# Positive parts of one batch's late queries: from ScalarE out of PSUM to GpSimd out of SBUF, with all engine lists made anew

## Chip, cores, metric

The kernel runs on one core of a Trainium2 chip. The metric is the device time of one execution in microseconds (us). The engines are named as in the profile: PE (TensorE), PEld (its weight loads), DVE (VectorE), ACT (ScalarE), POOL (GpSimd), SP (the queue that issues most transfers).

## What is computed

Block-sparse causal attention, followed by a two-layer feed-forward block with an ELU. Batch is 4, heads 8, sequence 768, head width 64, and keys come in 24 chunks of 32.

```python
k_min = np.min(k_chunks, axis=3); k_max = np.max(k_chunks, axis=3)
ub = np.sum(np.maximum(q * k_min, q * k_max), axis=-1)     # query against every chunk
ub = np.where(causal, ub, -1e9)
top_chunks = np.argsort(ub, axis=-1)[..., -6:]             # six chunks for each query
scores = where(selected and causal, q @ k.T / 8, -1e9)
x = softmax(scores) @ v                                    # (3072, 512)
h = x @ w_in                                               # (3072, 2048)
out = where(h > 0, h, exp(min(h, 0)) - 1) @ w_out          # (3072, 512)
```

The upper bound is computed as `q @ k_min + max(q, 0) @ (k_max - k_min)`, which is where the positive part of the queries comes from.

## The kernel before

Two heads make a pair; a batch has pairs 0 to 3, and two pairs make a quad, for which the chunks are selected together. Batches 1 to 3 are prepared a whole pair at a time (`pair_prep`). Batch 0 alone (`SPLIT`) is cut into two halves of 384 queries, so that work can begin early, and prepared by `first_prep(u, hf)`. For each pair and half it does the following. Keys and queries arrive in the tile `gT`, used here as a staging buffer. PE transposes them (L696) into PSUM banks, keys as `psH`, queries as `psMT`. ACT copies the keys to `lhs` (L706), DVE takes minima and maxima by chunk (L715) and their difference (L722). ACT copies the transposed queries to the SBUF tile `f` (L728) and writes their positive part to the tile `qa` (L732), both out of the PSUM bank, which is free after the second. For the first half the positive part has 192 columns (queries below 192 need no selection), for the second half 384. POOL casts the queries from `f` to bf16 in `rhs` (L748) and the values to `vext` (L739).

`quad_sel` then computes the bounds on PE out of `f`, `qa` and the chunk tiles (L782, into a two-bank PSUM tile `psS`). DVE transposes them (L798), takes the eight largest of each row (L810), compares (L815) and transposes back (L821). POOL copies the outcome into extra rows of `rhs` (L832, four copies for a quad, two for each pair). `pair_attend` computes scores (L874, with products for the triangular mask at L880), which carry the selection through these rows; a score tile of a half's queries waits for both copies of its pair. ACT makes exponentials (L901), PE multiplies by the values (L933), DVE normalizes (L946, L949), PE transposes (L982) and ACT copies to `xT` (L985). `mlp` is the feed-forward part: L1011, ELU on ACT and DVE (L1020 to L1054), L1070, L1079. There are two `psS` tiles, and four banks for `psH`, `psMT` and the other single-bank tiles together.

The order of work is fixed in advance. Each step is an operation with a number in the order of `add`, and `QUEUE` holds for each engine the list of these numbers, written out by hand. Each engine works through its list in order and waits, at each operation, for what that one needs. A small planner (`Plan`) walks these lists with assumed durations to choose buffers; its constants (`PHASE`, the durations given to `add`) reach the chip only through that choice. The eight weight loads are issued by POOL within its list (L570, L574), and they and their number stand in it like any other operation.

Numbers that the diff's lists show, for batch 0's second half: key transposes 169, 185, 203, 219 and query transposes 175, 191, 209, 225 for pairs 0 to 3; query copies 176, 192, 210, 226; positive parts 177, 193, 211, 227; casts of queries 178 and 179, 194 and 195, 212 and 213, 228 and 229. Bounds of the first half are 81 and 122, of the second 231 and 281. The two selection copies of pair 0 for the second half are 237 and 238, of pair 1 239 and 240. The first scores of pair 0's second half are 241, 243, 245, 247 and 249, by key block, with exponentials 242 to 250. Weight issues are 331 to 345. Loads on SP: 217 is the query load of pair 3's second half, 197 a key load of that half, 517 and 519 the first key and query load of batch 1 (four starts each), 17, 51, 201 and 167 value loads (three starts each).

Of the kernel before, what the change touches and what calls it, by code (L numbers as in the profile page):

```python
# [85 lines left out]
    ],  # L86
    "ACT": [
# [19 lines left out]
    ],  # L107
# [7 lines left out]
    ],  # L115
# [42 lines left out]
class Plan:  # L158
# [17 lines left out]
    def add(self, eng, dur, prio, emit, reads=(), writes=(), alloc=(), free=(), lat=None, tag="",  # L176
# [32 lines left out]
        o.users = []  # L209
        o.followers = []  # L210
        self.ops.append(o)
        return o

    WINDOW = 3.4133
    PHASE = 0.77
    ENOUGH = 0.43

    def clocked(self, r, dur, act):

        w = int(math.floor((r - self.PHASE) / self.WINDOW)) + 1  # L220
        warm = w > 0 and act[w - 1] >= self.ENOUGH * self.WINDOW
# [931 lines left out]
```

## Time and profile before

| | |
|---|---|
| runs (3) | median 268.44 us, from 268.43 to 268.44 |
| the profiled execution | 268.42 us, of which the span shown is 266.7 us |
| busy in the span | PE 256.0, DVE 211.6, ACT 195.8, POOL 118.0 us |
| the four instructions that move | L732 ACT, 128x384, 511 ns mean |

Times in the profile are from the start of the span. A row of the timeline gives start, length, engine, line, operation, output and inputs, and in brackets the idle time before it with what ended it. A row of groups gives count, busy time, mean duration in ns, then idle time ahead and what ended it. Names are the program's, without buffer numbers, so `rhs` is the bf16 query tile, `lhs` the key tile and `f` any of a pool of fp32 tiles.

### The profile page before, as it was taken

What the parts mean: (1) busy time and instruction counts of PE and PEld (TensorE: products, weight loads), DVE (VectorE), ACT (ScalarE), POOL (GpSimd) and SP (SyncE); (2) the same over time, 40 slices, a digit from 0 to 9 for tenths busy, and PEclk for the clock granted to TensorE, in tenths of its full rate; (3) what the DMA queues carried; (4) which work ended last, traced back from release to release, by engine and by line L of the source; (5) the groups of instructions that cost most, each with busy time, mean ns of one, the idle gap of its engine ahead of it and who ended that gap; (6) DMA issues with size and microseconds to landing.
All of it is one profiled execution on the core that took longest, in us unless ns stands there. A gap on an engine that the chain in (4) does not pass through costs nothing.

```text
span 266.7 us, 6618 instructions
## 1 busy us (share of the span) xinstructions
PE 256.0 (96%) x2393; PEld 159.4 (60%) x2420; DVE 211.6 (79%) x544; ACT 195.8 (73%) x363; POOL 118.0 (44%) x208
## 2 busy tenths in 40 slices
PE   4999999999999999999999999999999999999994
PEld 3887766755565556655565555655666555565543
DVE  4897999999999999899997858986779676227640
ACT  4899899955987789997899549787988842433421
POOL 2588774163896898952934157524250000000000
PEclk9999999999999999999999999999999999999999
DMA  6999999999998999999403561040102300210123
GB/s 206 272 238 155 205 194 202 196 147 177 198 153 134 163 204 159 152 167 186 106 7 77 175 172 18 15 125 15 58 11 59 116 2 0 79 42 0 39 81 118
DMA packets 121264, 32.15 MB, mean 121 GB/s; under 512 B 108304, under 2 KB 118288, under 8 KB 121232
## 3 DMA queue, kind: packets, MB, share of 16 engines
q1 hardware_dynamic: 115920, 26.75, 51.3%
q0 software_dynamic: 4224, 4.19, 10.0%
q10 hardware_dynamic: 1088, 0.79, 0.9%
q8 instruction: 19, 0.31, 0.5%
q14 instruction: 13, 0.11, 0.2%
HBM read 28.44 MB, written 7.47 MB: 135 GB/s over the span
## 4 chain that ended last, share of the span: by engine, by line
PE 83%; DVE 5%; ACT 5%; DMA 4%; issue 2%; SPq 0%; DVEq 0%; ACTq 0%
PE psH L1011 20%; PE psM L1070 20%; PE psS L874 11%; PE psS L1011 8%; PE psMT L1070 8%; PE psO L933 7%; PE psS L782 3%; DMA f<-in_v_dram 3%; PE psH L696 2%; PE psMT L696 2%; ACT pt L901 2%; DMA gT<-in_k_dram 1%; ACT lhs L706 1%; PE psT L982 1%; DVE thr L810 1%
## 5 line engine op out<-in xcount | busy, mean ns | idle before, releaser
L901 ACT ACTIVATE pt<-psS 128x768 bf16<-128x768 f32 (+1 forms) x120 | 89.1, 778 | 11.9 <-PE psS L874 7.3
L1011 PE MATMUL psH<-xT,w_in_sb 128*128 128x384 bf16 x384 | 75.0, 326 | 0.3
L1070 PE MATMUL psM<-w_out_sb,gT 128*128 128x512 bf16 x264 | 67.9, 379 | 1.3
L1011 PEld LDWEIGHTS <-w_in_sb 128*128 128x128 bf16 x512 | 47.6, 97 | 34.4 <-issue 1.4
L1070 PEld LDWEIGHTS <-gT 128*128 128x128 bf16 x400 | 37.8, 98 | 34.4 <-DVE gT L1054 0.5
L1020 ACT ACTIVATE f<-psH 128x384 f32<-128x384 f32 x96 | 47.8, 509 | 12.5 <-PE psH L1011 10.1
L920 POOL TENSOR_SCALAR_AFFINE_SELECT pt<-pt 128x512 bf16<-128x512 bf16 (+1 forms) x48 | 24.8, 529 | 69.0 <-ACT pt L901 61.9
L874 PE MATMUL psS<-rhs,lhs 88*128 88x384 bf16 (+4 forms) x304 | 54.2, 283 | 0.8 <-ACT pt L901 0.6
L874 PEld LDWEIGHTS <-lhs 88*128 88x128 bf16 x304 | 27.9, 97 | 15.4 <-ACT pt L901 1.9
L1049 DVE SCALAR_TENSOR_TENSOR t<-f,psH 128x384 bf16<-128x384 f32 x56 | 30.5, 546 | 6.3 <-ACT f L1020 5.8
L748 POOL CAST rhs<-f 64x768 bf16<-64x768 f32 (+1 forms) x40 | 27.9, 702 | 14.1 <-DVE f L633 6.6
L933 PEld LDWEIGHTS <-pt 128*128 128x128 bf16 x672 | 27.5, 98 | 7.5 <-issue 0.9
L1054 DVE SCALAR_TENSOR_TENSOR gT<-psH,t 128x384 bf16<-128x384 f32 x56 | 30.6, 551 | 1.2
L933 PE MATMUL psO<-vext,pt 128*128 128x65 bf16 x672 | 29.6, 194 | 0.2 <-DVE gT L1054 0.2
L748 POOL CAST lhs<-f 64x768 bf16<-64x768 f32 x24 | 19.7, 822 | 18.6 <-PE psS L874 12.3
L832 POOL COPY rhs<-selt 24x576 bf16<-24x576 bf16 (+2 forms) x40 | 22.7, 567 | 8.6 <-DVE selt L821 5.8
L1020 ACT ACTIVATE f<-psS 128x768 f32<-128x768 f32 x16 | 13.0, 811 | 18.0 <-PE psS L1011 17.9
L1028 DVE SCALAR_TENSOR_TENSOR gT<-f,psH 128x384 bf16<-128x384 f32 x40 | 21.4, 542 | 5.3 <-ACT psH L1025 5.3
L1011 PE MATMUL psS<-xT,w_in_sb 128*128 128x384 bf16 x128 | 22.6, 326 | 0.0
L1070 PE MATMUL psMT<-w_out_sb,gT 128*128 128x512 bf16 (+1 forms) x109 | 22.1, 348 | 0.2
L1025 ACT ACTIVATE psH<-psH 128x384 f32<-128x384 f32 x40 | 20.7, 520 | 0.0
L949 DVE TENSOR_TENSOR on<-psO,rc 128x384 bf16<-128x384 f32 x32 | 17.6, 554 | 0.8
(56 smaller groups left out, 270.9 us busy)
## 6 DMA issues: line engine op xcount, KB each, us to landing
out_dram<-osb SPq DMA_DIRECT2D x23, 256.0 KB, 2.5
f<-in_k_dram SPq DMA_DIRECT2D x48, 96.0 KB, 3.9
f<-in_q_dram SPq DMA_DIRECT2D x48, 96.0 KB, 3.8
f<-in_v_dram SPq DMA_DIRECT2D x24, 192.0 KB, 4.0
w_in_sb<-in_moe_w_in_dram POOLq DMA_DIRECT2D x4, 512.0 KB, 7.9
w_out_sb<-in_moe_w_out_dram POOLq DMA_DIRECT2D x4, 512.0 KB, 8.4
gT<-in_k_dram SPq DMA_DIRECT2D x8, 192.0 KB, 4.4
gT<-in_v_dram SPq DMA_DIRECT2D x12, 128.0 KB, 3.9
```

The source lines that it names most:

```text
L748: nc.gpsimd.tensor_copy(out=o, in_=i)
L832: eng.tensor_copy(out=dst.rearrange("c h (i two x) -> c h i two x", two=2, x=32)[:, :, :, odd, :], in_=tiles[st][r0:r0 + NCH, c0:c0 + n].r ...
L874: nc.tensor.matmul(p_s[:, hd, pc:pc + w], lhsT=tiles[pt_["kb"]][0:64 + NCH, hd, 128 * kb:128 * kb + 128], rhs=tiles[pt_["qb"]][0:64 + NCH, ...
L901: lambda bs=bs, pt=pt, wtot=wtot, lo=lo, at=at: nc.scalar.activation(out=tiles[pt][:, :, lo:lo + wtot], in_=tiles[bs[0]][:, :, at:at + wto ...
L920: nc.gpsimd.affine_select(out=a, in_=a, compare_op=AOT.is_ge, fill=0.0, base=0, pattern=pat, channel_multiplier=-1)
L933: nc.tensor.matmul(po[:, hd, qi, :], lhsT=tiles[pt][:, hd, off:off + 128], rhs=tiles[pt_["vx"]][:, 6 * hd + kb, :], start=(kb == 0), stop= ...
L1011: nc.tensor.matmul(o, lhsT=w_in_sb[:, kk, f0:f0 + 128], rhs=rhs, start=(kk == 0), stop=(kk == NKK - 1))
L1020: lambda e=e, view=view: nc.scalar.activation(out=halves(e)[:, 0:step], in_=view(), func=AF.Exp),
L1028: lambda e=e, view=view, fc=fc, gt=gt: nc.vector.scalar_tensor_tensor(out=tiles[gt][:, fc:fc + step, :], in0=halves(e)[:, 0:step], scalar= ...
L1049: lambda e=e, t=t, view=view: nc.vector.scalar_tensor_tensor(out=tiles[t][:, 0:step], in0=halves(e)[:, 0:step], scalar=1.0, in1=view(), op ...
L1054: lambda t=t, view=view, fc=fc, gt=gt: nc.vector.scalar_tensor_tensor(out=tiles[gt][:, fc:fc + step, :], in0=view(), scalar=0.0, in1=tiles ...
L1070: nc.tensor.matmul(pm, lhsT=tiles[gt][:, fc, 128 * tt:128 * tt + 128], rhs=w_out_sb[:, fc, x0:x1], start=(fc == 0), stop=(fc == NFC - 1))
```

## The change

For the second half of batch 0, the four positive parts (384 columns each) leave ACT. POOL makes them, by a `tensor_scalar` with a maximum against zero, out of the SBUF copy in `f` and no longer out of the PSUM bank. The bank is therefore free after ACT's copy. The first half's positive parts stay on ACT. The lists of all engines are written anew, and two of the planner's constants are changed.

```diff
-    PHASE = 0.77
+    PHASE = 1.2
...
-    add("ACT", 0.7, -9.0, c_econ, reads=["ident"], writes=["econ"])
+    add("ACT", 2.0, -9.0, c_econ, reads=["ident"], writes=["econ"])
...
+        lo = max(a, SEL0)
+        onpool = hf in (1,)
         add("ACT", act(HALF), pr + 0.05,
             lambda: nc.scalar.activation(out=tiles[qt][:, a:b], in_=ps(bq, None, None), func=AF.Copy),
-            reads=[bq[0]], writes=[qt], alloc=[qt])
-        lo = max(a, SEL0)
-        add("ACT", act(b - lo), pr + 0.05,
-            lambda: nc.scalar.activation(out=tiles[qa][:, lo - SEL0:b - SEL0], in_=ps(bq, None, None)[:, lo - a:HALF],
-                                         func=AF.Relu),
-            reads=[bq[0]], writes=[qa], alloc=[qa], free=bq)
+            reads=[bq[0]], writes=[qt], alloc=[qt], free=bq if onpool else [])
+        if onpool:
+            add("POOL", 0.13 + 0.00096 * (b - lo), pr + 0.05,
+                lambda: nc.gpsimd.tensor_scalar(out=tiles[qa][:, lo - SEL0:b - SEL0], in0=tiles[qt][:, lo:b],
+                                                scalar1=0.0, scalar2=None, op0=AOT.max),
+                reads=[qt], writes=[qa], alloc=[qa])
+        else:
+            add("ACT", act(b - lo), pr + 0.05,
+                lambda: nc.scalar.activation(out=tiles[qa][:, lo - SEL0:b - SEL0],
+                                             in_=ps(bq, None, None)[:, lo - a:HALF], func=AF.Relu),
+                reads=[bq[0]], writes=[qa], alloc=[qa], free=bq)
```

The heads of the lists, as far as batch 0's preparation goes (0 is the memset ahead of the identity, 6 clears the query rows, 1 makes the identity, 3 and 4 set POOL's constants):

```diff
 "DVE"
-        0, 6, 11, 9, 12, 8, 10, 22, 23, 38, 7, 39, 24, 40, 56, 57, 82, 72, 83, 73, 84, 172, 85, 58, 74, 188,
-        173, 123, 124, 189, 125, 126, 174, 222, 206, 190, 223, 207, 224, 208, 232, 233, 234, 235, 236, 521, 118,
+        6, 0, 7, 12, 9, 10, 8, 11, 38, 39, 40, 22, 23, 24, 56, 82, 83, 57, 72, 73, 84, 74, 58, 85, 172, 173,
+        188, 123, 124, 189, 125, 126, 222, 190, 174, 206, 521, 232, 207, 223, 233, 234, 235, 236, 224, 208, 118,
 "POOL"
-        1, 5, 4, 3, 28, 29, 44, 45, 46, 62, 30, 63, 179, 78, 80, 79, 87, 64, 178, 86, 89, 195, 129, 194, 128,
-        127, 88, 130, 213, 331, 229, 212, 228, 237, 238, 333, 335, 180, 239, 240, 337, 525, 214, 289, 288, 287,
+        3, 4, 1, 5, 28, 29, 44, 45, 30, 46, 179, 177, 62, 63, 178, 78, 79, 87, 80, 64, 86, 193, 194, 89, 88,
+        195, 130, 127, 129, 128, 213, 211, 229, 331, 228, 212, 227, 237, 238, 333, 335, 337, 239, 240, 214, 529,
 "ACT"
-        15, 33, 49, 67, 2, 20, 21, 36, 37, 26, 27, 42, 43, 54, 55, 60, 61, 176, 70, 71, 177, 76, 77, 170, 171,
-        186, 187, 220, 221, 192, 193, 91, 204, 92, 205, 107, 108, 94, 95, 132, 133, 210, 148, 149, 226, 211,
-        110, 111, 135, 227, 136, 151, 152, 242, 121, 248, 244, 246, 105, 146, 162, 266, 250, 348, 352, 353, 262,
+        15, 33, 49, 67, 2, 20, 21, 36, 37, 26, 27, 42, 43, 54, 55, 176, 60, 61, 70, 71, 76, 77, 170, 171, 192,
+        186, 187, 220, 91, 221, 204, 92, 205, 94, 107, 108, 95, 210, 226, 132, 133, 148, 149, 110, 111, 135,
+        136, 151, 152, 248, 242, 121, 244, 246, 105, 146, 162, 250, 266, 348, 352, 353, 262, 268, 372, 376, 292,
 "SP"
-        13, 31, 163, 47, 65, 165, 17, 215, 181, 51, 217, 183, 197, 199, 201, 167, 517, 519, 534, 536, 551, 565,
+        13, 31, 163, 47, 165, 65, 17, 199, 183, 181, 215, 51, 197, 517, 217, 201, 167, 519, 534, 536, 551, 548,
 "PE"
-        19, 35, 25, 41, 53, 59, 175, 69, 81, 75, 169, 90, 185, 219, 191, 122, 203, 209, 106, 93, 131, 225, 147,
-        231, 109, 134, 150, 112, 137, 115, 114, 116, 113, 117, 281, 241, 139, 96, 120, 98, 99, 100, 97, 101,
+        19, 35, 25, 41, 53, 175, 59, 81, 69, 75, 169, 191, 185, 219, 90, 122, 203, 209, 93, 106, 225, 231, 131,
+        147, 96, 100, 109, 134, 98, 150, 99, 112, 114, 113, 115, 116, 117, 281, 137, 247, 139, 241, 140, 120,
```

Behind these, and in the three later batches, the same operations stand in the lists in a partly different order.

149 rows, old and new, of the table QUEUE are left out of this document.

## The prediction

> **What bounds the kernel now.** I read the page first, then a table by stretches, then the chain of waits for the stretch the change touches.
>
> ```profile
> span 266.7 us, 6618 instructions
> ...
> PE 256.0 (96%) x2393; PEld 159.4 (60%) x2420; DVE 211.6 (79%) x544; ACT 195.8 (73%) x363; POOL 118.0 (44%) x208
> ```
>
> TensorE is busy for all but 10.7 us of the span. No edit here changes its work, so the time can only move by what happens to those gaps. The table by stretches shows where they are (columns after each window: its length, then busy us of PE, weight load, DVE, ACT, POOL, the granted clock, the DMA share, GB/s):
>
> ```profile
> 17.00:21.00 4.00, 3.51 (x49) 3.30 (x44) 3.79 (x19) 3.93 (x12) 2.90 (x8) 1.00 0.93 179
> 21.00:25.00 4.00, 3.59 (x71) 2.87 (x70) 2.72 (x19) 3.87 (x12) 3.55 (x8) 1.00 1.35 150
> 29.00:48.00 19.00, 18.80 (x196) 12.78 (x195) 17.99 (x45) 18.43 (x35) 11.32 (x19) 1.00 1.35 200
> 48.00:230.00 182.00, 180.40 (x1619) 106.88 (x1641) 158.39 (x389) 140.45 (x256) 87.26 (x138) 1.00 0.58 108
> ```
>
> From 17 to 25 us PE is idle for 0.49 + 0.41 = 0.9 us, from 29 to 230 us for 0.2 + 1.6 = 1.8 us in all. Batch 0's second half is prepared in that first stretch, so it decides. There ACT is at 3.93 and 3.87 of 4 us, but POOL is not free either: 2.90, then 3.55 of 4. The chain of that stretch (start, length, what) and ACT's waits from 9 to 48 us (total, times, longest):
>
> ```profile
> 17.43 0.49 ACT qa L732
> ...
> 23.20 0.06 PE psS L880
> ...
> 24.88 0.38 ACT qa L732
> 25.26 1.59 ACT pt L901 x3
> ...
> 26.89 0.50 PE psS L874 x2
> ```
> ```profile
> ACT pt L901 <- PE psS L874: 0.9, 2, 0.6
> ACT f L728 <- PE psMT L696: 0.4, 1, 0.4
> ```
>
> Two of the four removed instructions stand on the chain, with 0.49 + 0.38 = 0.87 us. That is the whole visible case for the change. The next question is what is late when they are gone, and that is read from POOL and from ACT's restart at 27.43:
>
> ```profile
> 11.71 0.50 POOL L739 CAST vext<-gT 128x384 bf16<-128x384 f32 x1 [0.89 <-DMA gT<-in_v_dram]
> ...
> 19.36 0.34 POOL L832 COPY rhs<-selt 24x192 bf16<-24x192 bf16 x1 [0.74 <-DVE km L722]
> ...
> 22.09 0.50 POOL L748 CAST rhs<-f 64x384 bf16<-64x384 f32 x1 [0.23 <-ACT f L728]
> 22.64 0.92 POOL L570 DMA_DIRECT2D w_in_sb<-in_moe_w_in_dram  x1
> 23.57 1.80 POOL L748 CAST rhs<-f 64x384 bf16<-64x384 f32 x3
> 25.68 1.05 POOL L832 COPY rhs<-selt 24x384 bf16<-24x384 bf16 x2 [0.31 <-DVE selt L821]
> ...
> 27.43 0.81 ACT L901 ACTIVATE pt<-psS 128x768 bf16<-128x768 f32 x1 [0.59 <-PE psS L874]
> ...
> 47.04 0.81 ACT L901 ACTIVATE pt<-psS 128x768 bf16<-128x768 f32 x1 [0.32 <-PE psS L874]
> ```
>
> The two copies that end at 25.68 + 1.05 = 26.73 put the selection rows of pair 0 beside its queries. The first score tile of the second half reads them and starts at 26.89. ACT's last exponential of the first half ends at 25.26 + 1.59 = 26.85. So POOL and ACT release those scores within 0.12 us of each other: POOL is a second chain beside the one printed, nearly as long. From 27.43 to 47.04 ACT has no wait in its list: its 0.9 us for scores are these 0.59 and 0.32, and the 0.4 belong to a query copy, which comes earlier. A delay at 27.43 is therefore carried whole to 47, where PE takes over, full to 230 us.
>
> **The change part by part.** *ACT loses four instructions.* The durations of what moves, and the nearest POOL operations, in three answers of groups (ACT 9 to 27.4 us, POOL 11.7 to 26.7 us, POOL whole run; busy, mean ns, then idle before):
>
> ```profile
> L732 ACT ACTIVATE qa<-psMT 128x384 f32<-128x384 f32 x4 | 2.0, 511 | 0.0
> ```
> ```profile
> L748 POOL CAST rhs<-f 64x384 bf16<-64x384 f32 x12 | 6.2, 528 | 0.6 <-ACT f L728 0.2
> L832 POOL COPY rhs<-selt 24x192 bf16<-24x192 bf16 x8 | 2.8, 344 | 1.2 <-DVE km L722 0.7
> L739 POOL CAST vext<-gT 128x384 bf16<-128x384 f32 x4 | 2.1, 515 | 1.0 <-DMA gT<-in_v_dram 0.9
> ...
> L832 POOL COPY rhs<-selt 24x384 bf16<-24x384 bf16 x2 | 1.0, 502 | 0.4 <-DVE selt L821 0.3
> ```
> ```profile
> L748 POOL CAST lhs<-f 64x768 bf16<-64x768 f32 x24 | 19.7, 822 | 18.6 <-PE psS L874 12.3 <-DVE rc L946 4.6 <-DVE f L615 0.9
> ```
>
> ACT is relieved of 4 x 0.511 = 2.0 us by duration.
>
> *POOL gains four.* The trace has no such operation on POOL. Below, it is bounded by the casts of as many columns, 0.515 to 0.528, above by the cast of twice the columns, 0.822. I take 0.53, the same column count and the same fp32 read. Nothing excludes a little less than 0.515, but a reading pass over 384 columns has no cheaper row.
>
> Now the sum on POOL. From 11.71 to 26.73 are 15.0 us. Busy in it are 6.2 + 2.8 + 2.1 + 1.0 + 0.92 (the first weight issue) = 13.0, so 2.0 us are open: 0.74 + 0.23 + 0.31 = 1.28 in three named waits and about 0.7 in short gaps between operations. In the new list the same 27 operations stand ahead of the end of those copies, and the four new ones too, each before them: 13.0 + 4 x 0.53 = 15.1 us. If every gap closes, they end at 11.71 + 15.1 = 26.8, 0.1 later than now; if only the named waits fill and the short gaps stay, at 27.5, 0.8 later. The start at 11.71 does not move, since it waits for a v load that keeps its place in SP's list. I take the middle, 0.45 us late. Three casts in a row already take 1.80 us, 0.60 each, so short gaps do not simply vanish.
>
> [...] The mean over twelve casts, 0.528, is the broader row, so I keep 0.53.
>
> *The selection does not come early enough either.* It runs query transposes on PE, bounds on PE, then DVE, then these copies. The new lists move pair 3's second-half query load behind another key load and behind the four starts of batch 1's first key load.
>
> ```profile
> 13.25 5.11 SPq L679 DMA_DIRECT2D gT<-in_v_dram  x6
> ...
> gT<-in_q_dram SPq DMA_DIRECT2D x4, 192.0 KB, 4.4
> ...
> 20.51 0.85 PE L696 MATMUL psMT<-ident_f,gT 128*128 128x128 f32 x6
> ...
> 22.71 0.58 DVE L798 STREAM_TRANSPOSE ubt<-psS 128x384 f32<-128x384 f32 x1 [1.16 <-PE psS L782]
> ```
>
> In SP's list nine starts lie between pair 0's first v load and the row at 13.25; this load becomes the thirteenth there. At the 5.11 / 6 = 0.85 us that starts take from 13.25 on, it goes out near 13.25 + 3 x 0.85 = 15.8 and lands 4.4 later, near 20.2. Its transposes stand ahead of the bounds of the first pairs in PE's list; they run at 20.51 today, so at most 0.3 us is won there. The bounds also win a score tile that stood between them and those transposes, out of the 1.16 us that DVE waits for them; but DVE now puts two more reductions between the transposition of the bounds and its maxima, and I set one against the other. So the selection reaches POOL at most 0.3 us before 25.68, and its copies end at 26.4 at best: POOL's queue is the later of the two.
>
> *The order of the scores.* The second half now begins with the tile of key block 3, which carries two mask products that the first tile of today has not: 2 x 0.06 = 0.12 us before ACT restarts.
>
> *The start.* DVE clears its query rows before the identity's memset, POOL its constants before the identity.
>
> ```profile
> 1.30 1.05 DVE L537 MEMSET rhs<- 32x192 uint32 x5
> ...
> 1.14 0.29 POOL L514 TENSOR_SCALAR_AFFINE_SELECT ident_f<-ident_f 128x128 f32<-128x128 f32 x1 [0.63 <-DVE ident_f L506]
> ...
> 3.96 2.79 PE L696 MATMUL psH<-ident_f,gT 128*128 128x128 f32 x12 [3.96 <-DMA gT<-in_k_dram]
> ```
>
> The identity is 1.05 us later, near 1.14 + 0.29 + 1.05 = 2.5. PE's first use waits for a load until 3.96, so this costs nothing; without that cover it would cost 1.05.
>
> *The weights.* Three of the four new operations and one more cast pass ahead of the first weight issue at 22.64: 4 x 0.53 less the waits 0.74 and 0.23 makes it 1.2 us later.
>
> ```profile
> w_in_sb<-in_moe_w_in_dram POOLq DMA_DIRECT2D x1, 512.0 KB, 6.8
> ...
> 31.44 1.71 PE L1011 MATMUL psH<-xT,w_in_sb 128*128 128x384 bf16 x8
> ```
>
> It lands at 22.64 + 6.8 = 29.4 now, at 30.6 then; its first reader starts at 31.44. Covered by 0.8 us, and priced at nothing.
>
> *Everything later* is reordered without a change of work. I take nothing; the bound on both sides is about 0.8, half of the 1.6 us that PE idles between 48 and 230, since a list can lose what it can win. The planner's changed constants issue nothing.
>
> **Sum.** 0.45 (POOL's copies) + 0.12 (mask products) = 0.57 us later at ACT's restart, carried to the end. The profiled execution took 268.42 us, 1.72 beyond its span and 0.02 below the median of the runs, 268.44. 268.42 + 0.57 = 268.99, so 269.0. By 0.2%, about what a measurement here can tell from no change, the border lies 0.54 us off.
>
> **The rivals.** *ACT's relief wins.* The copies end before ACT has finished the first half, which without the removed 0.87 us is near 26.0, because the short gaps close and the query load lands early. Then the scores follow ACT, and the gain is up to 0.87: 267.6. It decides if the copies end before some 26.4. For it: both chain rows. Against: 15.1 us of POOL work after 11.71. Chance 0.25.
>
> *It fits exactly.* POOL closes most of its gaps and the copies end near 26.8, with the mask products 0.2 us late: 268.6. Chance 0.28.
>
> *POOL's operation is dear.* At 0.822 each, or blocked by DVE, POOL ends 1.2 us later still: 268.99 + 1.2 = 270.2. It decides from about 0.6 us for one. Against: the casts of 384 columns take 0.515 and 0.528 on average. Chance 0.12, leaving 0.35 for the forecast.
>
> ```profile
> L722 DVE TENSOR_TENSOR km<-kx,km x8: 128/156/270, 10.2 to 21.4; 128x12 f32<-128x12 f32 x8
> ```
>
> One form on DVE takes 128 to 270 ns here, so something does hold it at times, but for a tenth of a microsecond. [...]
>
> **How the numbers follow.** Slower: 0.35 + 0.12 = 0.47; same 0.28; faster 0.25. The range goes from the full relief with a quarter of the later bound, 267.6 - 0.2 = 267.4, to the dear operation, 270.2.
>
> **What would show it.** Right: four 128x384 operations on POOL near 0.53, no 128x384 positive part on ACT, the pair 0 copies ending near 27.2, ACT idle over 1 us just before its restart near 28.0, and every later row of PE shifted by about 0.6. Wrong: copies ending by 26.4, ACT restarting before 27.4, or a POOL operation above 0.6. A new gap of PE after 48 us would make the time wrong with the mechanism right.

## Result and the profile after

The kernel after takes 271.61 us (median of five runs, 270.87 to 272.59), the kernel before 268.44 (268.43 to 269.11, five runs). The ratio is 1.0114, 95% interval 1.0099 to 1.013: slower by about 3 us. The forecast was 269.0 in a range up to 270.2. The direction held; the size was missed by a factor of more than five. The profiled execution took 272.59 us, 1.7 more than the span shown. Runs of this kernel come with a mean granted clock of 1.0 or of about 0.99, and the profiled one is of the second kind, which matters below.

The page of the kernel after: busy time by engine, the clock in 40 slices, and the shares of the chain that ended last.

```profile
span 270.9 us, 6646 instructions
...
PE 258.0 (95%) x2420; PEld 160.0 (59%) x2420; DVE 211.7 (78%) x544; ACT 194.8 (72%) x359; POOL 122.7 (45%) x212
...
PEclk9999799999999999999999999999999999999999
...
PE 85%; POOL 4%; ACT 4%; DVE 4%; issue 1%; DMA 1%; POOLq 0%; DVEq 0%; ACTq 0%
```

ACT has four instructions fewer and POOL four more, as the change says. POOL's busy time rose by 4.7 us, over twice the 2.1 us that the prediction gave it. A digit 7 stands in the fifth slice of the clock, where before every slice had 9.

The table by stretches of the kernel after (length, busy us of PE, weight load, DVE, ACT, POOL, granted clock, DMA share, GB/s):

```profile
17.00:21.00 4.00, 2.33 (x29) 2.06 (x27) 3.71 (x17) 3.04 (x9) 3.67 (x8) 1.00 0.88 178
21.00:25.00 4.00, 3.75 (x76) 2.96 (x75) 2.55 (x17) 2.90 (x9) 3.58 (x8) 1.00 0.94 162
...
48.00:230.00 182.00, 181.59 (x1673) 108.14 (x1671) 157.71 (x393) 143.26 (x261) 86.77 (x138) 1.00 0.60 111
```
```profile
27.00:29.00 2.00, 0.71 (x24) 0.29 (x15) 0.72 (x2) 0.61 (x2) 1.98 (x3) 1.00 0.88 114
29.00:31.00 2.00, 1.39 (x16) 0.84 (x17) 1.14 (x9) 0.03 (x1) 1.89 (x5) 0.92 1.24 190
31.00:33.00 2.00, 2.00 (x18) 1.34 (x16) 1.00 (x10) 1.91 (x3) 1.96 (x3) 0.50 1.40 211
33.00:35.00 2.00, 2.00 (x29) 1.64 (x28) 1.35 (x5) 1.72 (x3) 1.04 (x3) 0.72 1.27 181
```

The first two of these stretches in the kernel before:

```profile
27.00:29.00 2.00, 2.00 (x32) 1.53 (x32) 1.65 (x10) 1.57 (x3) 1.89 (x4) 1.00 1.37 210
29.00:31.00 2.00, 2.00 (x37) 1.78 (x36) 1.93 (x14) 2.00 (x4) 1.89 (x4) 1.00 1.37 198
```

From 27 to 31 us POOL alone is full (1.98 and 1.89 of 2), while ACT does 0.64 us in four. In the kernel before ACT did 3.57 us there and PE was full; ACT now has time and nothing to do. Then comes a second thing: the granted clock is 0.50 from 31 to 33 us. After 48 us PE is full again, so what is lost by 31 us is not won back.

POOL from 11.7 to 30 us in groups (busy, mean ns of one, idle before), and its timeline at the end of that stretch:

```profile
L756 POOL CAST rhs<-f 64x384 bf16<-64x384 f32 x12 | 6.2, 522 | 0.5
L735 POOL TENSOR_SCALAR qa<-f 128x384 f32<-128x384 f32 x4 | 4.7, 1167 | 0.3
L840 POOL COPY rhs<-selt 24x192 bf16<-24x192 bf16 x8 | 3.0, 370 | 0.4
L747 POOL CAST vext<-gT 128x384 bf16<-128x384 f32 x4 | 1.9, 503 | 0.7 <-DMA gT<-in_v_dram 0.7
L840 POOL COPY rhs<-selt 24x384 bf16<-24x384 bf16 x2 | 1.0, 500 | 0.1
L571 POOL DMA_DIRECT2D w_in_sb<-in_moe_w_in_dram x1 | 1.0, 997 | 0.0
```
```profile
25.98 1.00 POOL L571 DMA_DIRECT2D w_in_sb<-in_moe_w_in_dram  x1
27.02 0.95 POOL L756 CAST rhs<-f 64x384 bf16<-64x384 f32 x2
27.95 1.17 POOL L735 TENSOR_SCALAR qa<-f 128x384 f32<-128x384 f32 x1
29.18 1.04 POOL L840 COPY rhs<-selt 24x384 bf16<-24x384 bf16 x2
```

One positive part costs 1.167 us on POOL, as against 0.511 on ACT and the 0.53 assumed. The only named wait left on POOL is 0.7 us for a value load, at the start of the stretch, and the two selection copies end at 29.18 + 1.04 = 30.22 us, 3.5 later than the 26.73 of before. Who pays is seen in ACT's and PE's rows:

```profile
23.81 3.80 ACT L909 ACTIVATE pt<-psS 128x384 bf16<-128x384 f32 x8 [0.17 <-PE psS L888]
30.97 1.56 ACT L909 ACTIVATE pt<-psS 128x768 bf16<-128x768 f32 x2 [3.36 <-PE psS L888]
```
```profile
29.17 0.53 PE L790 MATMUL psS<-qa,km 64*32 64x192 f32 x8 [1.47 <-POOL qa L735]
...
30.28 0.32 PE L882 MATMUL psS<-rhs,lhs 88*128 88x384 bf16 x1 [0.44 <-POOL rhs L840]
```

ACT ends the first half at 23.81 + 3.80 = 27.61 and then idles 3.36 us. PE waits twice for POOL: first the bounds of the second quad, which stand ahead of the scores in its list, for pair 3's positive part, then the scores for the copies. The exponentials restart at 30.97 where they restarted at 27.43: 3.54 us later. The chain of waits lies on POOL, one weight issue in its queue included, from 18.22 to 30.24 us without a break.

### The profile page after: what moved, and what is told of

It is laid out like the page before. It is cut to its first block, busy times and chain, and to the rows that moved or that the text cites. A ratio compares the mean times of both kernels' runs of the same rounds, so it can differ in the third digit from the quotient of the medians.

```text
span 270.9 us, 6646 instructions
## 1 busy us (share of the span) xinstructions
PE 258.0 (95%) x2420; PEld 160.0 (59%) x2420; DVE 211.7 (78%) x544; ACT 194.8 (72%) x359; POOL 122.7 (45%) x212
## 4 chain that ended last, share of the span: by engine, by line
PE 85%; POOL 4%; ACT 4%; DVE 4%; issue 1%; DMA 1%; POOLq 0%; DVEq 0%; ACTq 0%
PE psM L1078 23%; PE psH L1019 21%; PE psS L882 12%; PE psS L1019 8%; PE psMT L1078 8%; PE psO L941 7%; PE psS L790 3%; ACT lhs L707 2%; PE psH L697 2%; PE psT L990 1%; POOL rhs L840 1%; POOL qa L735 1%; POOL rhs L756 1%; DMA gT<-in_k_dram 1%; DVE km L620 1%
## 5 line engine op out<-in xcount | busy, mean ns | idle before, releaser
L909 ACT ACTIVATE pt<-psS 128x768 bf16<-128x768 f32 (+2 forms) x120 | 89.4, 775 | 20.7 <-PE psS L882 11.6
L1078 PE MATMUL psM<-w_out_sb,gT 128*128 128x512 bf16 x288 | 71.5, 379 | 0.0
L1019 PEld LDWEIGHTS <-w_in_sb 128*128 128x128 bf16 x512 | 48.2, 97 | 35.5 <-issue 2.2
L941 PE MATMUL psO<-vext,pt 128*128 128x65 bf16 x672 | 30.3, 195 | 0.3 <-DVE on L957 0.3
L1046 DVE TENSOR_SCALAR t<-f 128x768 bf16<-128x768 f32 x16 | 8.9, 557 | 15.0 <-ACT f L1028 15.0
```

The source lines that it names most:

```text
L909: lambda bs=bs, pt=pt, wtot=wtot, lo=lo, at=at: nc.scalar.activation(out=tiles[pt][:, :, lo:lo + wtot], in_=tiles[bs[0]][:, :, at:at + wto ...
L941: nc.tensor.matmul(po[:, hd, qi, :], lhsT=tiles[pt][:, hd, off:off + 128], rhs=tiles[pt_["vx"]][:, 6 * hd + kb, :], start=(kb == 0), stop= ...
L1019: nc.tensor.matmul(o, lhsT=w_in_sb[:, kk, f0:f0 + 128], rhs=rhs, start=(kk == 0), stop=(kk == NKK - 1))
L1078: nc.tensor.matmul(pm, lhsT=tiles[gt][:, fc, 128 * tt:128 * tt + 128], rhs=w_out_sb[:, fc, x0:x1], start=(fc == 0), stop=(fc == NFC - 1))
```

## The experiments

**The price of the operation.** The kernel after with other forms in place of the maximum, one for each pair:

```diff
+            if u == 1:
+                nc.gpsimd.tensor_scalar(out=o, in0=i, scalar1=1.0, scalar2=None, op0=AOT.mult)
+            elif u == 2:
+                for x in range(0, HALF, HALF // 2):
+                    nc.gpsimd.tensor_scalar(out=o[:, x:x + HALF // 2], in0=i[:, x:x + HALF // 2], ...)
+            elif u == 3:
+                nc.gpsimd.tensor_copy(out=o, in_=i)
+            else:
+                nc.gpsimd.tensor_scalar(out=o, in0=i, scalar1=0.0, scalar2=None, op0=AOT.max)
```

> The changed kernel with another form for three of the four pairs: pair 0 the maximum over 384 columns as it is, pair 1 a product by 1.0 over 384 columns (no positive part), pair 2 the maximum in two pieces of 192, pair 3 a plain copy (no positive part). If the price lies in the form of the instruction (tensor with a scalar, fp32 to fp32): the product costs 1.17 as the maximum does, the copy 0.5, and two pieces show the share that is per instruction: near 0.62 each if little is fixed, near 0.8 each if 0.4 is fixed. If it is the maximum alone, the product costs 0.5. If it is the fp32 output, the copy costs 1.1 too.

Groups of POOL from 11.7 to 30 us (L743 is the maximum, L736 the product, L739 the maximum in two halves, L741 the plain copy):

```profile
L766 POOL CAST rhs<-f 64x384 bf16<-64x384 f32 x12 | 5.9, 503 | 0.5
...
L739 POOL TENSOR_SCALAR qa<-f 128x192 f32<-128x192 f32 x2 | 1.3, 686 | 0.1
L743 POOL TENSOR_SCALAR qa<-f 128x384 f32<-128x384 f32 x1 | 1.2, 1179 | 0.1
L736 POOL TENSOR_SCALAR qa<-f 128x384 f32<-128x384 f32 x1 | 1.2, 1175 | 0.1
...
L741 POOL COPY qa<-f 128x384 f32<-128x384 f32 x1 | 0.5, 503 | 0.0
```

The product by one costs what the maximum costs, and a plain fp32 copy of the same tile costs 0.503. So, for these two operations, neither the maximum nor the fp32 output nor the 128 partitions is dear, but the form: a tensor with a scalar operand. The halves give its slope: (1179 - 686) / 192 = 2.57 ns for a column, and about 0.19 us fixed. The casts of before, 0.822 for 768 columns, with the 0.503 here for 384, have 0.83 ns for a column and about 0.18 us fixed. By this estimate from two lengths of each, the two forms differ in the time for a column by a factor of three (2.57 / 0.83). One run of this kernel took 270.71 us.

Whether work on DVE beside it is what makes the operation dear can be read from the kernel after. Its four positive parts took 1.164 to 1.171 us, and the last of them, from 27.95 to 29.12, ran while DVE did nothing: DVE's row before it ends at 27.75, and the next one is this.

```profile
29.77 0.58 DVE L806 STREAM_TRANSPOSE ubt<-psS 128x384 f32<-128x384 f32 x1 [2.02 <-PE psS L790]
```

The spacing of starts says the same as the reported length: the operations behind the four start 1.11 to 1.23 us after them.

**The change at the assumed price.** The kernel after with a plain copy in place of the maximum; the positive part is left out.

```diff
-                lambda: nc.gpsimd.tensor_scalar(out=tiles[qa][:, lo - SEL0:b - SEL0], in0=tiles[qt][:, lo:b],
-                                                 scalar1=0.0, scalar2=None, op0=AOT.max),
+                lambda: nc.gpsimd.tensor_copy(out=tiles[qa][:, lo - SEL0:b - SEL0], in_=tiles[qt][:, lo:b]),
```

> The changed kernel with a plain copy on POOL in place of the maximum, so the positive part is left out; all else is the same. If the price of the operation is all: a copy takes about 0.53 us, and the time is what the prediction gave for that price, 269.0 (268.5 to 269.5), selection copies of pair 0 ending near 27.2. If any fourth-part of POOL's list at this place is too much, or the new lists lose by themselves, it stays above 270.5.

Measured 269.02 us (268.34 to 271.49, twelve runs), ratio 1.0012 [0.9992, 1.0031] to a before of 268.86 on that chip. POOL's group, its copies, and ACT's restart:

```profile
L735 POOL COPY qa<-f 128x384 f32<-128x384 f32 x4 | 2.0, 504 | 0.2
```
```profile
26.73 1.05 POOL L839 COPY rhs<-selt 24x384 bf16<-24x384 bf16 x2
```
```profile
28.47 1.51 ACT L908 ACTIVATE pt<-psS 128x768 bf16<-128x768 f32 x2 [1.05 <-PE psS L887]
```

All of the change is in this kernel but the price, and the ratio falls from 1.0114 to 1.0012. At the assumed price the forecast's range would have held. That the median falls on the forecast's 269.0 is in part luck: the kernel before took 268.86 us here and 268.44 there. The interval, from 0.2 us below the kernel before to 0.8 above it, does not tell the forecast's 0.57 from nothing.

**The two parts alone.** First the new lists and constants with the positive parts left on ACT, right behind each query copy; then the positive parts on POOL in the lists of before:

```diff
-        onpool = hf in (1,)
+        onpool = hf in ()
```

> The new lists with the four positive parts back on ACT, each right behind its query copy. If POOL's new operation is the cause (1.167 us each in the profile of after, where 0.53 was assumed), the loss goes with it: 268.4 plus or minus 0.8, the selection copies of pair 0 end near 26.7, PE's granted clock stays at 1.0 around 31 us. If the new lists themselves are the cause (pair 3's query load behind batch 1's first key load, the changed order of bounds and scores), it stays above 270.5.

```diff
+        onpool = hf in (1,)
...
-            reads=[bq[0]], writes=[qt], alloc=[qt])
+            reads=[bq[0]], writes=[qt], alloc=[qt], free=bq if onpool else [])
+        if onpool:
+            add("POOL", 0.13 + 0.00096 * (b - lo), pr + 0.05, lambda: nc.gpsimd.tensor_scalar(...), ...)
```

> The lists and constants of before, with the four positive parts on POOL, each behind the first cast of its pair. If POOL's operation is the cause: 4 x 1.167 = 4.7 us of new work against 1.3 to 2.0 us of open time ahead of pair 0's selection copies, so they end 2.7 to 3.4 us later than 26.73 and the time is 271.1 to 271.9, or about 1.2 more where the clock drops for a stretch. If the new lists are the cause: 268.4 to 269.2.

The lists alone: 270.06 us (269.5 to 270.33, six runs), ratio 1.0044 [1.0027, 1.0061]. The move alone: 272.51 (271.01 to 273.36, six runs), ratio 1.0124 [1.0093, 1.0155]. DVE and ACT with the lists alone, and DVE in the kernel after:

```profile
23.18 0.54 DVE L705 TENSOR_REDUCE kx<-psH 128x12 f32<-128x384 f32 x1
...
23.65 0.54 DVE L705 TENSOR_REDUCE kx<-psH 128x12 f32<-128x384 f32 x1
...
26.02 0.58 DVE L818 STREAM_TRANSPOSE selt<-selv 128x384 bf16<-128x384 bf16 x1
```
```profile
28.87 1.51 ACT L898 ACTIVATE pt<-psS 128x768 bf16<-128x768 f32 x2 [0.75 <-PE psS L877]
```
```profile
25.70 0.58 DVE L829 STREAM_TRANSPOSE selt<-selv 128x384 bf16<-128x384 bf16 x1
```

The move alone costs about as much as the whole change, and the plain copy, which has all but the price, costs almost nothing: the loss is POOL's operation. Four of the six runs of the move alone have a mean clock of 0.994; the two at 1.0 took 271.01 and 271.12 us, still 2.2 us above before.

The lists alone came between the two expectations, about 1.2 us above before. Both releases of the scores are late there. The copies end 0.99 us later, at 27.72: the selection's last transposition starts at 26.02 instead of 25.04, because the two reductions that the new list puts inside the selection, at 23.18 and 23.65, take 0.93 us there. In the kernel after that hides behind POOL, whose copies start 2.9 us after the selection is there (25.70 + 0.58). But ACT is later still: it ends its first half at 28.12 instead of 26.84, and before that it has one long wait.

```profile
16.51 0.49 ACT L729 ACTIVATE qa<-psMT 128x384 f32<-128x384 f32 x1 [1.21 <-PE psS L779]
```

Here the positive part of pair 1 waits until PE has made bounds of the first half. The kernel after has no such operation on ACT, so this wait belongs to the place that the experiment gave the positive part. The 1.2 us are therefore not the price of the lists by themselves; how they divide was not tried.

**ACT's relief without POOL's price.** The lists of before, with the positive parts on DVE: all four, and then pairs 1 and 3 only, two of the four.

```diff
+        onpool = hf == 1 and u in (0, 1, 2, 3)        # the second kernel: u in (1, 3)
...
+            add("DVE", 0.26, pr + 0.05, lambda: nc.vector.tensor_scalar(..., op0=AOT.max), ...)
```

> Lists and constants of before, all four positive parts on DVE instead (from the copy in SBUF), placed behind its other work of the same pair, the last two ahead of and behind the bounds of the first quad. If what counts is the engine that makes them and its open time, DVE's one open wait of 1.16 us near 22 us takes most of four operations of about 0.3 us, ACT loses 2.0 us, and the time is 267.7 to 268.4. If any change of these lists costs as the new lists did with ACT (+1.2), it is 269 or more.

> As e5, with only the two positive parts that stood on the chain of waits (pairs 1 and 3, 0.49 and 0.38 us) on DVE; the other two stay on ACT. If the chain is read rightly, it gains what e5 gains, up to 0.87 us less what DVE gives back: 267.6 to 268.4. If ACT's pace is not what releases the second half's scores, no change: 268.4 to 268.9.

Four: 269.0 us (268.68 to 272.01, 13 runs), ratio 1.0005 [0.9992, 1.0018]. Two: 268.7 (268.65 to 270.59, twelve runs), ratio 1.0004 [0.9988, 1.002], to a before of 268.73. The gain did not come. The profile of the first is of its 272.01 us run, the only one of the 13 with a lowered clock (0.994), and is not used for this. POOL and ACT in the second:

```profile
26.12 1.04 POOL L829 COPY rhs<-selt 24x384 bf16<-24x384 bf16 x2 [0.77 <-DVE selt L818]
```
```profile
23.40 3.07 ACT L898 ACTIVATE pt<-psS 128x384 bf16<-128x384 f32 x6
27.74 0.81 ACT L898 ACTIVATE pt<-psS 128x768 bf16<-128x768 f32 x1 [1.27 <-PE psS L871]
```

ACT now ends its first half at 26.47 instead of 26.84, and idles 1.27 us instead of 0.59 before it restarts. The copies wait for DVE, which has the new work, and end at 27.16, 0.43 later than before. They release the same scores, so what ACT gained bought nothing.

**Shortening the other chain.** In the lists of before, the bounds of the first quad go ahead of a first-half score tile, and pair 0's copies ahead of two casts. One kernel does only that; the other also puts the positive parts of pairs 0 to 2 on DVE.

```diff
 PE:   ... 225,
-      147, 231,
+      231, 147,
       109, ...
 POOL: ... 229,
-      212, 228, 237, 238,
+      237, 238, 212, 228,
       333, ...
```

> Lists of before with only the selection of pair 0 brought forward, the positive parts all on ACT as before. Theory 'two chains of equal length': the copies end near 26.1, but ACT still ends its first half near 26.85, so its restart moves by 0.1 us at most (27.3 to 27.4) and the time is 268.3 to 268.6, no change. Rival 'the selection alone decides': ACT restarts near 26.9 and the time is 267.8 to 268.2, as with the positive parts moved too.

> Lists of before with two things: the positive parts of pairs 0, 1 and 2 on DVE (pair 3's stays on ACT), and the selection of pair 0 brought forward (on PE the bounds of the first quad ahead of one first-half score tile, on POOL pair 0's two selection copies ahead of two casts). Theory 'two chains of equal length release the scores, so that both must be shortened together': the copies end near 26.1 instead of 26.73, ACT's first half ends near 26.0 instead of 26.85, ACT restarts near 26.9 instead of 27.43, and the time is 267.8 to 268.2. Rival 'the selection alone decides': the same time as the run that only brings the selection forward, whatever ACT does. Rival 'what ACT gains at its restart is lost later': restart near 26.9, time 268.4 to 268.8.

The selection alone: 269.06 us (268.94 to 270.08, twelve runs), ratio 1.0018 [1.0006, 1.003]. Both: 269.34 (268.7 to 270.37, twelve runs), ratio 1.0017 [1.0003, 1.003], to a before of 268.76. Both expectations missed. ACT and PE in the first:

```profile
22.75 0.66 ACT L891 ACTIVATE pt<-psS 128x384 bf16<-128x384 f32 x2 [0.76 <-PE psS L870]
...
28.08 0.81 ACT L891 ACTIVATE pt<-psS 128x768 bf16<-128x768 f32 x1 [0.59 <-PE psS L864]
```
```profile
22.97 0.42 PE L864 MATMUL psS<-rhs,lhs 88*128 88x192 bf16 x3 [0.26 <-DVE ubt L788]
```

The bounds and the scores share the two `psS` tiles. With the bounds first, the scores come later: ACT starves for 0.76 us, and PE then waits until DVE has read the bounds. The copies end 0.34 us sooner, ACT's first half 0.65 later, and the restart is 0.65 later. In the second kernel the copies end at 27.13, later than before, so it never made the case that it was to test: whether shortening both chains at once gains is left open.

All the kernels together, from the same rows of each profile (copies end, ACT's first half ends, ACT restarts; the last column is the time of the profiled execution):

| kernel | copies | ACT | restart | restart less the later | us |
|---|---|---|---|---|---|
| before | 26.73 | 26.84 | 27.43 | 0.59 | 268.42 |
| two parts on DVE | 27.16 | 26.47 | 27.74 | 0.58 | 268.68 |
| selection earlier | 26.39 | 27.49 | 28.08 | 0.59 | 269.48 |
| both chains | 27.13 | 27.97 | 28.56 | 0.59 | 269.59 |
| plain copy | 27.78 | 27.41 | 28.47 | 0.69 | 269.10 |
| lists alone | 27.72 | 28.12 | 28.87 | 0.75 | 270.02 |
| four forms (above) | 29.37 | 27.35 | 30.06 | 0.69 | 270.71 |
| wait filled (below) | 29.61 | 27.00 | 30.30 | 0.69 | 271.05 |
| move alone | 29.77 | 26.74 | 30.53 | 0.76 | 272.59 |
| after | 30.22 | 27.61 | 30.97 | 0.75 | 272.59 |
| after, again (below) | 29.81 | 27.60 | 30.67 | 0.86 | 272.15 |
| four parts on DVE | 30.52 | 29.86 | 31.10 | 0.58 | 272.01 |

The restart comes 0.6 to 0.9 us after the later of the two, whichever it is: copies in eight rows, ACT in four. And the time follows the restart nearly one to one, within some 0.4 us, except in the move alone and the two profiles of the kernel after, which are about 1.1, 0.6 and 0.5 us dearer than their restart says. In these three the granted clock falls shortly before ACT restarts (1.00 from 27 to 29 us, then 0.75, 0.92 and 0.79 from 29 to 31, in the order of the table). With four parts on DVE it falls near 18 us (0.81 from 17 to 19, 0.50 from 19 to 21), and the restart already holds what that costs.

**The clock.** To see whether this rest is the granted clock, PE is kept busy while it waits: the first pass of the second quad's bounds is repeated four times more, with the same values. The kernel after ran unchanged beside it.

```diff
-                for w in range(2):
+                for w, alone in ([(0, True)] * 4 if g == 1 and c0 and not whole else []) + [(0, False), (1, False)]:
...
-                                                 start=(w == 0), stop=(w == 1))
+                                                 start=(w == 0), stop=(w == 1 or alone))
```

> The changed kernel, with PE repeating the first pass of the second quad's bounds four times more (the same values written again), in the stretch where it waits for POOL's last positive part. If the clock drop near 31 us comes from PE's idle stretch, the granted clock stays at 1.0 there and the runs near 272.5 vanish: 270.8 to 271.6, no run above 272. If the drop has another cause, some runs stay at clock 0.99 and above 272. If the loss is PE's idle time as such, filling it changes nothing else.

> The changed kernel once more, on the same chip as e7, for its spread: runs of two kinds, 270.8 to 271.7 with clock 1.0 and about 1.2 us more with clock 0.99.

Filled: 271.46 us (271.05 to 273.05, six runs), ratio 1.0106 [1.008, 1.0133]. Unchanged: 271.68 (271.06 to 272.59, six runs), ratio 1.0108 [1.0085, 1.0132]. Stretches of the filled kernel, as above:

```profile
25.00:29.00 4.00, 3.76 (x120) 2.98 (x119) 1.52 (x6) 2.00 (x5) 3.89 (x6) 1.00 0.92 136
29.00:33.00 4.00, 3.36 (x49) 2.43 (x46) 3.20 (x20) 2.70 (x5) 3.82 (x7) 1.00 1.30 185
```

With PE busy 3.76 of 4 us the clock stays at 1.00, and none of its six runs has a mean clock below 0.998. Of the eleven runs of the unchanged kernel, five have 0.991 to 0.993 (271.78 to 272.59 us, median 272.34) and six 0.998 or more (270.87 to 271.61, median 271.41): where it falls, the drop costs about 0.9 us (in the move alone 1.6, 272.69 beside 271.07). The medians of the two kernels are too near each other to show it, and one filled run of 273.05 us at clock 0.998, above the 272 that was expected, is unexplained. So the drop explains most of the spread and the profiled run, not the slowdown: the runs without it are still nearly 3 us above before. That PE's wait is what brings the drop fits these runs, but six filled runs are too few to exclude chance.

## Why the prediction was wrong

**The step that failed** is "POOL gains four", sized at 0.53 us each from the casts, with 0.822 as its upper end. It measured 1.167. A cast reads and writes as many columns, but it is another form with another cost for a column (0.83 ns as against 2.57), and no row of the profile before showed the form used here. The bound from above was none: a row of the same engine with twice the columns bounds only its own form. The cast row that was nearest by shape was the wrong neighbour.

**The sum around it held**, nearly. POOL's busy time ahead of the copies' end was put at 15.1 us; the groups now add to 17.8, and 4 x (1.167 - 0.53) = 2.55 of the 2.7 between is the price. Put into the prediction's own sum, 268.42 + 0.57 + 2.55 = 271.54 us; the median is 271.61. That this agrees to 0.1 us is closer than the spread of the runs allows to claim, and the start of the stretch, put at 11.71, came at 11.33. The rival "POOL's operation is dear" had this mechanism, but its price, 0.822, gave 270.2 and ended the range there. Its other half, "blocked by DVE", is not shown: with DVE idle beside it the operation took 1.17 us all the same.

**POOL as the second chain** was right: the copies and ACT's first half are two releases of the same scores, as the table shows in both directions. The copies' end (27.2 predicted) and the restart (28.0) are 30.22 and 30.97. The plain copy, without the price, has 27.78 and 28.47, so most of both errors, 2.4 and 2.5 us, is the price. The other 0.6 us of the copies is the choice of the middle between 26.8 and 27.5: POOL has no named wait from 11.81 to 27.78 there, and the short gaps between its operations stayed, as in the later of the two cases.

**"I set one against the other"** was wrong by 0.7 to 1 us. What the bounds win by leaving a score tile behind was to pay for two reductions inside the selection. The bounds reach DVE only 0.15 us earlier in the kernel after (22.56 instead of 22.71), and the last transposition starts at 25.70, 0.66 later than before, with the lists alone 0.98 later. POOL's lateness hides it. It is no part of the plain copy's time either: the selection is ready at 26.47 there, and POOL comes to it at 26.73.

**Mask products**: 0.12 predicted. The restart comes 0.58 or 0.59 us after the later release in the kernels that begin with the tile of before and whose clock does not fall there, 0.69 and 0.75 in those with the new lists: 0.10 to 0.17, as said.

**ACT's relief wins** did not come true in any kernel. It needs copies that end before 26.4 with ACT ending near 26.0. With two parts on DVE ACT ended at 26.47, but the copies at 27.16, and the ratio is 1.0004. With the selection earlier the copies ended at 26.39, but ACT at 27.49. In the kernel after, ACT is relieved of four operations and still ends at 27.61, because it waits for scores. A kernel with both ends early was not made.

**Start, query load, weights.** The rows that answer:

```profile
2.25 0.29 POOL L515 TENSOR_SCALAR_AFFINE_SELECT ident_f<-ident_f 128x128 f32<-128x128 f32 x1 [0.23 <-DVE ident_f L507]
...
4.08 2.79 PE L697 MATMUL psH<-ident_f,gT 128*128 128x128 f32 x12 [4.08 <-DMA gT<-in_k_dram]
...
20.77 0.84 PE L697 MATMUL psMT<-ident_f,gT 128*128 128x128 f32 x6 [0.76 <-DMA gT<-in_q_dram]
...
36.04 1.46 PE L1019 MATMUL psH<-xT,w_in_sb 128*128 128x384 bf16 x8
```

The identity ends at 2.54, near the predicted 2.5, and PE still waits for a load until 4.08: hidden, as said. Pair 3's query load is used at 20.77, where 20.2 was predicted, and PE now waits 0.76 us for it; POOL is later. The weight issue went out 3.3 us later, 25.98 instead of 22.64, and not 1.2; but its first reader moved from 31.44 to 36.04 too, so the cover grew with the cost.

**Carried whole to the end** was right, to 0.4 us where the clock does not fall. The bound of 0.8 for later reordering came from 1.6 us in which PE idles after 48 us. The stretch here leaves 0.41 us open. The page of before counts 2393 matmuls and 2420 weight loads, the page after 2420 of both: at least a part of that idle time was 27 missing records, and the bound was too wide.

**Not foreseen** was the clock. PE now waits for POOL, and in five of eleven runs the clock fell (a mean of 0.991 to 0.993 over the span).

## What to carry to other kernels

Price a moved operation by a row of the same form on the target engine, and where there is none, say that the upper end is open: a row of the same shape in another form was short by a factor of 2.2. Before relieving the busiest engine, look for the second release of the instruction that it feeds; where both came within a tenth of a microsecond, as here, relief of one bought nothing, and load on the other was paid nearly in full. A queue that looks 44% busy over the run was 87% busy where it mattered (13.0 of 15.0 us).

## What the runs showed of the hardware

A tensor with a scalar on POOL took 2.57 ns for a column of fp32 beside 0.83 for a copy or a cast, at nearly the same fixed cost (about 0.19 and 0.18 us); both are estimates from the lengths for 192 and 384, and for 384 and 768 columns. DVE idle beside it made it no faster (1.17 us). The same operation on DVE took 0.35 and 0.66 us in the kernel with two of them, and 0.42 on average in the kernel with four, where about 0.3 was expected.

In the profiled run of the kernel after PE was busy for 1.37 of the 3 us from 27 to 30, with a longest pause of 1.47 us. The granted clock was then 0.50 for about 3.4 us: windows of 0.1 us read 1.00 from 30.5 to 30.6, 0.50 from 30.7 to 30.8 and still 0.50 from 34.0 to 34.1, and from 34.2 to 40 us it is 1.00. With these two values alone the share of a stretch at 0.50 is (1 - clock) / 0.5, and the table gives the same: (1 - 0.92) x 2 / 0.5 + 2.0 + (1 - 0.72) x 2 / 0.5 = 0.32 + 2.0 + 1.12. The second profile of this kernel has 0.79, 0.50 and 0.86 in the three stretches of 2 us from 29 to 35, which is 0.84 + 2.0 + 0.56 = 3.4 again, after PE had been busy for 0.94 of the 2 us from 27 to 29. From 18 to 21 us in the first of these profiles PE was busy for 1.43 of 3 us, and the clock stayed at 1.00. What sets the drop off and what sets its length is not shown by these runs.

The profiled run with four parts on DVE, 3 us above its median, has a drop of the same length (with 0.84 from 21 to 23 us: 0.76 + 2.0 + 0.64) at another place, right after PE had been idle half the time:

```profile
15.00:17.00 2.00, 0.91 (x9) 0.64 (x6) 1.69 (x7) 1.83 (x5) 1.71 (x5) 1.00 0.91 264
17.00:19.00 2.00, 1.09 (x6) 0.78 (x6) 0.33 (x1) 0.29 (x1) 1.16 (x4) 0.81 0.85 195
19.00:21.00 2.00, 2.00 (x39) 1.57 (x39) 0.87 (x9) 0.87 (x2) 0.50 (x1) 0.50 0.91 195
```
